# An attention and FFN kernel: tail keys as side-by-side 64-row matmuls, and the slot loop as one written-out list

## The chip, the cores and the metric

The kernel runs on one core of a Trainium2 chip. The metric is the device time of one execution in microseconds (us), lower is better. The core has TensorE (matrix products; the profile shows its weight loads apart, as PEld), VectorE (DVE), ScalarE (ACT), GpSimd (POOL) and SyncE (SP). POOL, SP and ACT also issue DMA transfers here. Each engine works through its own instructions in order and waits on semaphores for the others. TensorE reads SBUF and writes PSUM, eight banks of 2 KB per partition; ScalarE and VectorE read PSUM and write SBUF.

## What is computed

Self-attention over 8 batches and 8 heads of 576 tokens and 64 dimensions, with a bias that depends on the distance of two tokens, followed by a bilinear feed-forward network (FFN) over all 4608 tokens:

```
scores = q @ k.T / 8 + bias[|i - j|]          # per batch and head, 576 x 576
attn   = softmax(scores);  x = attn @ v       # back to [8*576, 512]
out    = ((x @ w_a) * (x @ w_b)) @ w_out      # 512 -> 1536 -> 512
```

## The kernel before

**Pairs and tails.** Two heads are worked together as a pair; pair p belongs to batch p // 4, so there are 32. The 576 tokens are four blocks of 128 ("main") and a tail of 64. Scores are made transposed, keys on partitions and queries along the free dimension. The bias enters as a product: `ex` (line 436) takes the exponential of the scores on ScalarE, and `mul` (442) multiplies it by the exponential of the bias on VectorE.

**Scores of a pair** (`qk`, line 408). For each main key block two products with 64 contracted rows, one per head, write the two banks of a `ps_sc` tile; there are two such tiles, used in turn, so a new block needs an older one to have been read by `ex`. For pairs from 8 on (`shared`), the call for blocks 2 and 3 also makes the scores of the tail queries against the main keys ("rows"), in eight 64-row products of 64 columns, into two banks: `trb`, otherwise used for transposes, and one of pool `ps_av`. `ex_rows` (428) reads them in two activations. `qk_tail` (484) makes the tail keys' scores in a third `ps_sc` tile: one product of 512 columns for the main queries and one of 128 for the tail queries. Its operand `z` holds the two heads as blocks on a diagonal, with zeros elsewhere, so that both heads go through all 128 rows at once. `ex_tail` (508) and `mul_tail` (526) follow.

**Products with V** (`av`, 559). The accumulators of a pair fit pool `ps_av`, one bank, in two rounds: query blocks 0 to 2, then block 3 and the tail. For each block, `av_mm` (563) first multiplies the tail keys' weights, both heads on 128 partitions, with `vt`, which is 130 columns wide and zero where head and partition do not match; then eight products of 65 columns over the main keys. For the query tail the main keys take four products of 130 columns. The 65th column of V is one, so that it sums the weights. `av_norm` (583) divides on VectorE into `XG`, and `t_x` (600) turns `XG` by DMA transposes on SP into `xn`, the FFN's input.

**FFN.** A chunk is 512 tokens. `ff_in` (639) makes `pa` or `pb`, four products of 512 columns; `ff_ha` copies `pa` out on ScalarE, `ff_g` multiplies it with `pb` on VectorE into `g`. `ff_o_mm` (673) makes a third of an output block in four products, `ff_o_out` (682) copies it out on ScalarE and issues its store from there. These go through the two banks of pool `ps_ff` in turn. A "unit" is one `ff_in` with what follows, or one third of an output block.

**Order of the work.** Every engine's instructions stand in the order in which the code issues them. Batches 0 and 1 (pairs 0 to 7) are in a written-out list, `opening` (737). From line 868, slots 8 to 32 follow: slot s makes the scores of pair s and the products with V of pair s - 1, and spreads nine FFN units over marks `U` between these steps. Loads of later batches are issued on POOL at fixed slots (`load_half`, `load_vt`), transposes of q and k on SP (`t_half`). What is left of the FFN follows the last slot. The chunk worked on lags the attention by a batch; the opening ends with the first three output units of chunk 0.

Of the kernel before, what the change touches and what calls it, by code (L numbers as in the profile page):

```python
# [13 lines left out]
def kernel(  # L14
# [33 lines left out]
    wrk = ctx.enter_context(tc.tile_pool(name="wrk", bufs=2))  # L48
    atp = ctx.enter_context(tc.tile_pool(name="atp", bufs=10))
    ps_sc = ctx.enter_context(tc.tile_pool(name="ps_sc", bufs=2, space=bass.MemoryType.PSUM))  # L50
    ps_av = ctx.enter_context(tc.tile_pool(name="ps_av", bufs=1, space=bass.MemoryType.PSUM))
    ps_tr = ctx.enter_context(tc.tile_pool(name="ps_tr", bufs=1, space=bass.MemoryType.PSUM))
    ps_ff = ctx.enter_context(tc.tile_pool(name="ps_ff", bufs=2, space=bass.MemoryType.PSUM))

    ctx.enter_context(tc.manual_schedule())

# [40 lines left out]
    tl = [wpool.tile([128, H // 2, 2, 128], BF16, name=f"tl{i}") for i in range(2)]  # L97
    vm = [wpool.tile([128, H, NM, Dh + 1], BF16, name=f"vm{i}") for i in range(2)]
    vt = [wpool.tile([128, 2, H // 2, Dh + 1], BF16, name=f"vt{i}") for i in range(2)]

    QT = [wpool.tile([128, NM, 128], BF16, name=f"QT{i}") for i in range(4)]
    KT = [wpool.tile([128, NM, 128], BF16, name=f"KT{i}") for i in range(4)]
# [69 lines left out]
    def load_vt(b):  # L172
        for hh in range(2):
            nc.gpsimd.dma_start(  # L174
                out=vt[b % 2][64 * hh:64 * hh + 64, hh, :, 0:Dh],
                in_=v[b, hh:H:2, SM:S, :].transpose([1, 0, 2]))

    def load_half(b, g):
# [37 lines left out]
    def pad_ones(i):  # L216
        nc.vector.memset(vt[i][0:64, 0, :, Dh:Dh + 1], 1.0)
        nc.vector.memset(vt[i][64:128, 1, :, Dh:Dh + 1], 1.0)
        nc.vector.memset(vm[i][:, :, :, Dh:Dh + 1], 1.0)

    def pad_x(i, eng):
        pad(eng, XG[i][64:128, 4, :, :], 64, 128)
# [182 lines left out]
    def shared(p):  # L405
        return p >= 8

    def qk(p, t0, ts=None):
        qT, kT, _ = operands(p)
        st[p].setdefault("at", [None] * NM)  # L410
        for t in ts or (t0, t0 + 1):
            ps = ps_sc.tile([128, 2, 512], FP32, tag="sc", name=f"qk{p}_{t}")
            for hh in range(2):
                r = slice(64 * hh, 64 * hh + 64)
                nc.tensor.matmul(out=ps[:, hh, :], lhsT=kT[r, t, :], rhs=qT[r, :, :],  # L415
                                 start=True, stop=True)
            st[p]["ps", t] = ps
        if shared(p) and t0 == 2:
            z = operands(p)[2]
            rows = (trb.bitcast(FP32), ps_av.tile([128, 512], FP32, tag="av", name=f"qr{p}"))  # L420
            for t in range(NM):
                for hh in range(2):
                    r = slice(64 * hh, 64 * hh + 64)
                    nc.tensor.matmul(out=rows[hh][:, ST * t:ST * t + ST], lhsT=kT[r, t, :],  # L424
                                     rhs=z[r, 0, ST * hh:ST * hh + ST], start=True, stop=True)
            st[p]["rows"] = rows

    def ex_rows(p):
        st[p]["att"] = at = att[p % 2]
        for hh in (1, 0):  # L430
            nc.scalar.activation(
                out=at[:, 0:512].rearrange("p (t h c) -> p h t c", h=2, t=NM)[:, hh, :, :],
                in_=st[p]["rows"][hh][:, 0:256].rearrange("p (t c) -> p t c", t=NM),
                func=ACTF.Exp, scale=scale)

    def ex(p, t):
        ps = st[p]["ps", t]
# [46 lines left out]
    def qk_tail(p):  # L484
        qT, kT, z = operands(p)
        ps = ps_sc.tile([128, 2, 512], FP32, tag="sc", name=f"qkt{p}")
        if shared(p):
            nc.tensor.matmul(out=ps[:, 0, :], lhsT=z[:, 1, :], rhs=qT[:, :, :], start=True, stop=True)  # L488
            nc.tensor.matmul(out=ps[:, 1, 0:2 * ST], lhsT=z[:, 1, :], rhs=z[:, 0, :],  # L489
                             start=True, stop=True)  # L490
            st[p]["ps"] = (ps, None)
            return
        for t in range(NM):
            nc.tensor.matmul(  # L494
                out=ps[:, 0, 2 * ST * t:2 * ST * t + 2 * ST],
                lhsT=kT[:, t, :], rhs=z[:, 0, :], start=True, stop=True)
        n = main_tail(p)
        nc.tensor.matmul(out=ps[:, 1, 0:n], lhsT=z[:, 1, :], rhs=qT[:, (SM - n) // 128:, :],
                         start=True, stop=True)
        pt = ps[:, 1, n:n + 2 * ST] if n < SM else tr_half().bitcast(FP32)[:, 0:2 * ST]  # L500
        nc.tensor.matmul(out=pt, lhsT=z[:, 1, :], rhs=z[:, 0, :], start=True, stop=True)  # L501
        st[p]["ps"] = (ps, pt)


    def main_tail(p):
        return SM // 2 if p < 4 else SM

    def ex_tail(p):
        ps, pt = st[p]["ps"]
        n = main_tail(p)  # L510
        at = att[p % 2]
        m = 512 + n
        st[p]["att"] = at
        if shared(p):
            nc.scalar.activation(out=at[:, 512:m + 2 * ST],  # L515
                                 in_=ps[:, :, :].rearrange("p a x -> p (a x)")[:, 0:SM + 2 * ST],
                                 func=ACTF.Exp, scale=scale)
            return
        if n < SM:
            m += 2 * ST  # L520
        else:
            nc.scalar.activation(out=at[:, m:m + 2 * ST], in_=pt, func=ACTF.Exp, scale=scale)
        nc.scalar.activation(out=at[:, 0:m], in_=ps[:, :, :].rearrange("p a x -> p (a x)")[:, 0:m],
                             func=ACTF.Exp, scale=scale)

    def mul_tail(p):
        if not shared(p):
            mul_rows(p)
        at, wt = st[p]["att"], Wt_sb[:, p % 4, :]
        o = 512 + main_tail(p) - 128  # L530
        nc.vector.tensor_tensor(out=at[:, o:o + 256], in0=at[:, o:o + 256], in1=wt[:, 255::-1], op=MULT)

    def mul_rows(p):
        at, w = st[p]["att"], W_sb[p % 4]
        x = at[:, 0:512].rearrange("p (t h c) -> p h t c", h=2, t=NM)
        rev = w[:, :, ST - 1::-1]
        e = bass.AP(tensor=rev.tensor, offset=rev.offset,
                    ap=[rev.ap[0], rev.ap[1], [1, NM], rev.ap[2]])
        nc.vector.tensor_tensor(out=x, in0=x, in1=e, op=MULT)

    def weights(p, t, hh, jq):
        if p >= 4:
# [2 lines left out]
        return st[p]["at", jq // 2, t // 2][:, hh, o:o + 128]  # L545

    def weights_last(p, t):
        return st[p]["att"][:, 2 * ST * t:2 * ST * t + 2 * ST]

    def weights_tail(p, jq):  # L550
        if jq == 4:
# [4 lines left out]
        o = 512 + 128 * (jq if p >= 4 else jq - 2)  # L556
        return st[p]["att"][:, o:o + 128]

    def av(p, jqs):
        av_mm(p, jqs)  # L560
        av_norm(p, jqs)

    def av_mm(p, jqs, pool=None, tag="av"):
        b, hp = divmod(p, 4)
# [298 lines left out]
    for token in opening.split():  # L863
        step(token)
    pad_tl(1)

    load_slot = {bb: 9 if bb == 3 else 12 if bb == 4 else 4 * bb - 5 for bb in range(3, B)}
    for s in range(8, NP + 1):
        new = s < NP
        U = "unit"  # L870
        A = lambda *jq: (lambda: av(s - 1, jq) if s > 8 else None)
        steps = []
        if new:
            steps += [lambda: (qk(s, 0), ex(s, 0))]
        if new:
            head = [U, lambda: ex(s, 1), A(0, 1, 2), U, lambda: mul(s, 0), U,
                    lambda: mul(s, 1)]
            late = [A(3, 4), lambda: t_x(s - 1), U]
            if s == 8:
                late = [U]  # L880
            pair = [lambda: v_next(s), lambda: (qk(s, 2), ex(s, 2), ex_rows(s)), U,
                    lambda: ex(s, 3), U, lambda: mul(s, 2), lambda: mul_rows(s)]
            tail = [lambda: (qk_tail(s), ex_tail(s)), U, U, lambda: mul_tail(s)]
            if s % 4 == 0:
                steps += head + late + [U] + pair + [lambda: mul(s, 3)] + tail
            else:
                steps += head + pair + late + [U, lambda: mul(s, 3)] + tail
        else:
            ff["late"] = True
            steps += [A(0, 1, 2), U, U, U, A(3, 4), lambda: t_x(s - 1, (0, 1, 2)), U, U, U,  # L890
                      lambda: t_x(s - 1, (3, 4)), U, U, U]
        b = s // 4 + 1
        if s % 4 == 2 and b < B:
            t_half(b, 0)
        if s % 4 == 0 and 2 <= b - 1 < B:
            t_half(b - 1, 1)
        if s % 4 == 1 and 2 <= b < B:
            load_vt(b)
        for bb in range(3, B):
            for g in range(2):  # L900
                if s == load_slot[bb] + (2 - (bb < 5)) * g:
                    load_half(bb, g)
        quota = 9
        seen, put = 0, 0
        nu = sum(1 for x in steps if x is U)
        for x in steps:
            if x is U:
                seen += 1
                n = (quota * seen + nu - 1) // nu - put
                put_units(n)  # L910
                put += n
            else:
                x()
    put_units(len(units) - nxt)


# [28 lines left out]
```

## Time and profile before

| | |
|---|---|
| time, median of 3 runs (lowest, highest) | 413.77 us (413.61, 414.19) |
| span of the profiled execution | 412.1 us |
| TensorE busy | 401.5 us, 97% |
| VectorE, ScalarE, GpSimd busy | 240.6, 252.0, 131.4 us |
| 896 products `av<-vm,at` of 65 columns (line 578) | 41.2 us |
| 152 products `av<-vt,att` of 130 columns (line 568) | 33.6 us |
| 128 products `av<-vm,att` of 130 columns (line 572) | 12.6 us |

The profile is of one execution. The page gives that execution's time as its span, from the first to the last instruction; the timed executions have some 1.7 us more around it. The page of a profile lists busy times and instruction counts by engine, the chain of work that ended last, and groups of instructions by line, engine and operands; a timeline lists instructions in order with their start and duration in us. A product's duration includes its way through the array after its last column, so that products one after another overlap in the records, and the distance of two starts is what one of them costs TensorE. Where two products are recorded as starting a few ns apart, they run together. A few matmul records are missing from the trace: 152 of the 160 tail products of line 568, for example.

### The profile page before, as it was taken

The numbers are of one execution on the slowest core, as the hardware profiler recorded it, in microseconds if no ns is written. First come the engines' busy times: TensorE is split into PE (matmuls) and PEld (weight loads), VectorE is DVE, ScalarE is ACT, GpSimd is POOL, SyncE is SP. The second block draws the span as 40 slices with busy tenths as digits, with TensorE's granted clock in tenths as the row PEclk, the third lists the DMA queues.
The fourth block names the chain that finished last, engine by engine and source line by source line (L and its number), as shares of the span: only waits on it lengthen the run. The fifth ranks groups of instructions, "written<-read, shape, count | busy, mean of one in ns | idle before, by whom it ended". The sixth has DMA issues, their size and how long they took to land.

```text
span 412.1 us, 8718 instructions
## 1 busy us (share of the span) xinstructions
PE 401.5 (97%) x3420; PEld 209.6 (51%) x3471; DVE 240.6 (58%) x568; ACT 252.0 (61%) x386; POOL 131.4 (32%) x188
## 2 busy tenths in 40 slices
PE   7999999999999999999999999999999999999996
PEld 3476656455554555455445555555445454444443
DVE  4799997366755765476646764567547652421320
ACT  5898992577748665667557765767476642322321
POOL 5966466887029400960069004300000000000000
PEclk9999999999999999999999999999999999999999
DMA  9999999999969924994199908960520012002004
GB/s 152 185 204 197 206 137 148 166 184 131 91 127 157 141 40 91 151 127 94 35 159 150 120 17 136 117 92 17 117 67 17 16 40 78 0 5 98 2 2 102
DMA packets 135962, 42.36 MB, mean 103 GB/s; under 512 B 113544, under 2 KB 131176, under 8 KB 135920
## 3 DMA queue, kind: packets, MB, share of 16 engines
q0 software_dynamic: 81120, 19.88, 54.9%
q1 hardware_dynamic: 49456, 12.61, 19.9%
q10 hardware_dynamic: 5344, 9.31, 7.1%
q8 instruction: 27, 0.44, 0.5%
q14 instruction: 15, 0.12, 0.1%
HBM read 39.23 MB, written 9.45 MB: 118 GB/s over the span
## 4 chain that ended last, share of the span: by engine, by line
PE 95%; DMA 1%; ACT 1%; issue 1%; DVE 0%; ACTq 0%; SPq 0%
PE pb L642 23%; PE pa L642 23%; PE po L679 22%; PE av L578 8%; PE qk L415 7%; PE av L568 2%; PE av L572 2%; PE qkh L455 1%; PE qkt L488 1%; DMA xn<-in_k_dram 1%; PE trb L330 1%; PE trb L424 1%; PE trk L330 1%; ACT ath L461 0%; PE qkt L494 0%
## 5 line engine op out<-in xcount | busy, mean ns | idle before, releaser
L439 ACT ACTIVATE at<-qk 128x1024 bf16<-128x1024 f32 x112 | 113.4, 1029 | 27.4 <-DMA out_dram<-ob 10.3
L652 DVE TENSOR_TENSOR g<-pb,ha 128x512 bf16<-128x512 f32 (+1 forms) x114 | 75.6, 663 | 74.8 <-PE pb L642 58.5
L642 PE MATMUL pb<-xn,wb 128*128 128x512 bf16 (+1 forms) x440 | 111.1, 368 | 0.8
L642 PE MATMUL pa<-xn,wa 128*128 128x512 bf16 (+1 forms) x440 | 110.8, 368 | 0.7
L649 ACT ACTIVATE ha<-pa 128x512 f32<-128x512 f32 (+1 forms) x114 | 66.3, 581 | 67.6 <-PE pa L642 63.8
L679 PE MATMUL po<-wo,g 128*128 128x512 bf16 x403 | 95.5, 379 | 0.8
L444 DVE TENSOR_TENSOR at<-at,W 128x1024 bf16<-128x1024 bf16 x112 | 75.0, 685 | 22.4 <-ACT at L439 22.3
L642 PEld LDWEIGHTS <-wa 128*128 128x128 bf16 x456 | 41.2, 98 | 46.6 <-issue 6.8
L642 PEld LDWEIGHTS <-wb 128*128 128x128 bf16 x456 | 40.6, 98 | 42.9 <-issue 4.7
L679 PEld LDWEIGHTS <-g 128*128 128x128 bf16 x420 | 38.8, 98 | 44.9 <-issue 2.5
L684 ACT ACTIVATE ob<-po 128x512 f32<-128x512 f32 x34 | 20.4, 600 | 40.2 <-PE po L679 30.1
L578 PE MATMUL av<-vm,at 128*128 128x65 bf16 x896 | 41.2, 193 | 0.0
L578 PEld LDWEIGHTS <-at 128*128 128x128 bf16 x896 | 37.4, 97 | 6.1
L174 POOL DMA_DIRECT2D vt<-in_v_dram x12 | 7.4, 622 | 101.9 <-PE av L572 101.1
L136 POOL DMA_DIRECT2D qn<-in_q_dram x48 | 36.6, 825 | 9.2 <-PE trb L501 6.9
L589 DVE RECIPROCAL rc<-av 128x6 f32<-128x6 f32 (+1 forms) x64 | 11.9, 186 | 45.7 <-PE av L578 41.1
L145 POOL DMA_DIRECT2D kn<-in_k_dram x48 | 36.2, 800 | 2.6 <-DMA qn<-in_q_dram 1.6
L568 PE MATMUL av<-vt,att 128*128 128x130 bf16 x152 | 33.6, 221 | 0.2
L415 PE MATMUL qk<-QB,KB 64*128 64x512 bf16 x192 | 29.1, 381 | 0.3
L591 DVE TENSOR_TENSOR XG<-av,rc 128x384 bf16<-128x384 f32 (+2 forms) x64 | 27.2, 425 | 2.2
L515 ACT ACTIVATE att<-qkt 128x640 bf16<-128x640 f32 x24 | 16.8, 701 | 13.0 <-PE qkt L489 13.0
L568 PEld LDWEIGHTS <-att 128*128 128x128 bf16 x152 | 14.9, 98 | 6.4
(105 smaller groups left out, 322.8 us busy)
## 6 DMA issues: line engine op xcount, KB each, us to landing
out_dram<-ob ACTq DMA_DIRECT2D x31, 256.0 KB, 2.9
vn<-in_v_dram POOLq DMA_DIRECT2D x16, 256.0 KB, 5.7
kn<-in_k_dram POOLq DMA_DIRECT2D x48, 64.0 KB, 4.9
qn<-in_q_dram POOLq DMA_DIRECT2D x48, 64.0 KB, 4.1
wa<-in_moe_w_a_dram POOLq DMA_DIRECT2D x3, 512.0 KB, 8.9
wb<-in_moe_w_b_dram POOLq DMA_DIRECT2D x3, 512.0 KB, 8.3
wo<-in_moe_w_out_dram POOLq DMA_DIRECT2D x1, 1536.0 KB, 15.7
xn<-XG SPq DMA_TRANSPOSE x52, 3.5
```

The lines of the kernel that those rows point to most:

```text
L136: nc.gpsimd.dma_start(out=by_tile(qn[b % 2])[:, h0 // 4, t, :, :], in_=q[b, h0:h1, 128 * t:128 * t + 128, :].transpose([1, 0, 2]))
L145: nc.gpsimd.dma_start(out=by_tile(kn[b % 2])[:, h0 // 4, t, :, :], in_=k[b, h0:h1, t:SM:NM, :].transpose([1, 0, 2]))
L415: nc.tensor.matmul(out=ps[:, hh, :], lhsT=kT[r, t, :], rhs=qT[r, :, :], start=True, stop=True)
L439: nc.scalar.activation(out=at[:, :, :], in_=ps[:, :, :], func=ACTF.Exp, scale=scale)
L444: nc.vector.tensor_tensor(out=at[:, :, :], in0=at[:, :, :], in1=w[:, :, S - 1 + t:S - 1 + t - SM:-1], op=MULT)
L568: nc.tensor.matmul(out=pav[:, slot, :, :], lhsT=weights_tail(p, jq), rhs=vt[i][:, :, hp, :], start=True, stop=True)
L578: nc.tensor.matmul(out=pav[:, slot, hh, :], lhsT=weights(p, t, hh, jq), rhs=vm[i][:, 2 * hp + hh, t, :], start=False, stop=True, skip_grou ...
L591: nc.vector.tensor_tensor(out=xg[:, jqs[0]:jqs[0] + m, :, :], in0=pav[:, 0:m, :, 0:Dh], in1=rc[:, 0:m, :].unsqueeze(3).to_broadcast([128, ...
L642: nc.tensor.matmul(out=ps[:, 0:n], lhsT=w[df // 4][:, mc, 128 * (df % 4):128 * (df % 4) + 128], rhs=xn_sb[mc][:, 512 * c + lo:512 * c + lo ...
L649: nc.scalar.activation(out=ha[:, 0:n], in_=ff["pa", df, lo][:, 0:n], func=ACTF.Copy)
L652: nc.vector.tensor_tensor(out=g_sb[df][:, lo:lo + n], in0=ff["pb", df, lo][:, 0:n], in1=ff["ha", df, lo][:, 0:n], op=MULT)
L679: nc.tensor.matmul(out=po[:, :], lhsT=g_sb[df][:, 128 * tt:128 * tt + 128], rhs=wo_sb[:, df, :], start=(df == 0), stop=(df == NDF - 1))
```

## The change

1. **Tail keys, pairs from 8 on.** The tails of V go to a buffer of their own, `vc`, in which each head has its 64 partitions and 65 columns, without zeros. `av_tails` makes the tail products as ten 64-row products of 65 columns, the two heads alternating, and `av_main` follows with 40 products of 65 columns over the main keys; the query tail's four products of 130 columns are now eight of 65. All five query blocks of both heads are accumulated in one round in `xav`, two banks, one for each head. `av_out` and `av_out_last` divide all of it: one reciprocal, one product and two small ones, where two rounds took six instructions.
2. **Rows.** The tail queries' scores against the tail keys leave `qk_tail` and join the rows as a fifth pair of 64-row products. The rows are made after the first two score blocks, not the last two, and read by one activation instead of two.
3. **Banks.** Pools `ps_av` and `ps_tr` are closed after the opening, and their two banks become the tile `xb`, which holds in turn the rows, the accumulators `xav` and, for the last pair, the transposes.
4. **Order.** The slot loop becomes a list of single steps over the four slots of a batch, `steady`, the same for batches 2 to 7. A token names a step and the slot within the batch: Q0 and Q2 score blocks (Q0 with the rows, Q2 with the tail products of the pair before), QZ the tail keys' scores, E, ER, EZ exponentials, M, MR, MZ products with the bias, AV, N, NT products with V and division of the pair before, X its transposes; FA, FB, HA, G, FO, HO the parts of FFN units. For chunk 0 the tokens FO0, FO1, FO2 and HO0 are passed over.

```diff
@@ qk, qk_tail, ex_rows
-        if shared(p) and t0 == 2:
+        if shared(p) and t0 == 0:
             z = operands(p)[2]
-            rows = (trb.bitcast(FP32), ps_av.tile([128, 512], FP32, tag="av", name=f"qr{p}"))
-            for t in range(NM):
+            for t in range(NM + 1):
                 for hh in range(2):
                     r = slice(64 * hh, 64 * hh + 64)
-                    nc.tensor.matmul(out=rows[hh][:, ST * t:ST * t + ST], lhsT=kT[r, t, :],
+                    nc.tensor.matmul(out=xb[:, hh, ST * t:ST * t + ST],
+                                     lhsT=z[r, 1, :] if t == 0 else kT[r, t - 1, :],
                                      rhs=z[r, 0, ST * hh:ST * hh + ST], start=True, stop=True)
...
-            nc.tensor.matmul(out=ps[:, 1, 0:2 * ST], lhsT=z[:, 1, :], rhs=z[:, 0, :],
-                             start=True, stop=True)
...
+    def av_tails(p):
+        b, hp = divmod(p, 4)
+        for jq in range(5):
+            for hh in range(2):
+                r = slice(64 * hh, 64 * hh + 64)
+                nc.tensor.matmul(out=xav[:, hh, jq, :], lhsT=st[p]["att"][r, 128 * jq:128 * jq + 128],
+                                 rhs=vc[b % 2][r, hp, :], start=(jq == 0), stop=True,
+                                 skip_group_check=True)
+
+    def av_main(p):
+        b, hp = divmod(p, 4)
+        for t in range(NM):
+            for jq in range(5):
+                for hh in range(2):
+                    nc.tensor.matmul(out=xav[:, hh, jq, :],
+                                     lhsT=weights(p, t, hh, jq) if jq < 4 else weights_last(p, t),
+                                     rhs=vm[b % 2][:, 2 * hp + hh, t, :], start=False, stop=True,
+                                     skip_group_check=True)
...
@@ slot loop
-        quota = 9
-        ...
+    steady = """
+        Q0.0 E0.0 FO0 FO1 QZ.0 E1.0 FO2 ER.0 M0.0 EZ.0 Q2.0 E3.0 E2.0 AV.0 N.0 NT.0 V.2 FO3 HO0 MR.0
+        M3.0 FO4 FO5 FO6 HO1 Q0.1 FO7 MZ.0 E0.1 E1.1 X.0 FO8 FO9 ER.1 FO10 FO11 M2.0 HO2 V.0 HO3
+        M1.0 FA0 FB0 HA0 G0 QZ.1 M1.1 FA1 FB1 EZ.1 HA1 G1 Q2.1 FA2 M0.1 FB2 HA2 E2.1 G2 M2.1 AV.1
+        E3.1 FA3 N.1 NT.1 HA3 FB3 Q0.2 FA4 E0.2 HA4 MZ.1 G3 FB4 X.1 QZ.2 FA5 E1.2 EZ.2 ER.2 G4 HA5
+        FB5 MR.1 Q2.2 FA6 M0.2 G5 MR.2 FB6 HA6 M3.1 AV.2 G6 E3.2 E2.2 M1.2 FA7 HA7 FB7 N.2 NT.2 Q0.3
+        G7 FA8 E0.3 HA8 FB8 E1.3 MZ.2 ER.3 QZ.3 M2.2 EZ.3 G8 FA9 X.2 HA9 FB9 M3.2 Q2.3 FA10 G9 FB10
+        MR.3 AV.3 HA10 E3.3 MZ.3 E2.3 M1.3 FA11 G10 N.3 NT.3 FB11 M0.3 X.3 M3.3 HA11 M2.3 G11
+    """.split()
...
+    for b in range(2, B):
+        c = b - 2
+        for token in steady:
+            kind, _, r = token.partition(".")
+            if r:
+                pair_step(kind, 4 * b + int(r))
+                continue
+            if token == "FA0":
+                c += 1
+            if c == 0 and token in ("FO0", "FO1", "FO2", "HO0"):
+                continue
+            ff_step(c, token)
+
+    p = NP - 1
+    ff["late"] = True
+    av_tails(p)
+    av_main(p)
+    put_units(1)
+    av_out(p)
+    put_units(1)
+    av_out_last(p)
+    put_units(2)
+    t_x(p, (0, 1, 2))
+    put_units(1)
+    t_x(p, (3, 4))
     put_units(len(units) - nxt)
```

## The prediction

> **What bounds the kernel now.** I read the page's busy shares first, then the chain that ended last, a table of stretches for the slot loop, the timeline of TensorE over one slot, and the timelines of TensorE and ScalarE at 73 us, where the slot loop begins.
>
> ```profile
> PE 401.5 (97%) x3420; PEld 209.6 (51%) x3471; DVE 240.6 (58%) x568; ACT 252.0 (61%) x386; POOL 131.4 (32%) x188
> PE 95%; DMA 1%; ACT 1%; issue 1%; DVE 0%; ACTq 0%; SPq 0%
> 180.00:200.00 20.00, 19.84 (x173) 9.91 (x175) 13.48 (x29) 14.12 (x22) 2.49 (x4) 1.00 0.64 81
> ```
>
> The third line is a stretch of the slot loop: TensorE 19.84 of 20.00 us at granted clock 1.00, VectorE 13.48, ScalarE 14.12. TensorE alone sets the time there: the first score products of two slots start at 116.18 and 127.19, 11.01 us apart. What the change is worth is what it takes off TensorE in a slot, less whatever idle time the new order opens. Busy time counts a product's drain too, so prices are start-to-start:
>
> ```profile
> 204.99 0.81 PE L679 MATMUL po<-wo,g 128*128 128x512 bf16 x3
> 205.63 0.22 PE L568 MATMUL av<-vt,att 128*128 128x130 bf16 x1
> 205.69 0.42 PE L578 MATMUL av<-vm,at 128*128 128x65 bf16 x8
> 205.95 0.22 PE L568 MATMUL av<-vt,att 128*128 128x130 bf16 x1
> ...
> 210.22 0.59 PE L679 MATMUL po<-wo,g 128*128 128x512 bf16 x2
> 210.74 0.60 PE L415 MATMUL qk<-QB,KB 64*128 64x512 bf16 x4
> 211.19 0.19 PE L424 MATMUL trb<-ZB,KB 64*128 64x64 bf16 x1
> 211.19 0.19 PE L424 MATMUL qr<-ZB,KB 64*128 64x64 bf16 x1
> ...
> 211.27 0.19 PE L424 MATMUL trb<-ZB,KB 64*128 64x64 bf16 x1
> 211.28 0.19 PE L424 MATMUL qr<-ZB,KB 64*128 64x64 bf16 x1
> 211.40 1.90 PE L679 MATMUL po<-wo,g 128*128 128x512 bf16 x8
> 213.14 0.38 PE L488 MATMUL qkt<-QB,ZB 128*128 128x512 bf16 x1
> 213.35 0.22 PE L489 MATMUL qkt<-ZB 128*128 128x128 bf16 x1
> 213.41 0.38 PE L679 MATMUL po<-wo,g 128*128 128x512 bf16 x1
> ```
>
> A 130-column tail product takes 0.06 (205.63 to 205.69), the eight 65-column ones after it (205.95 - 205.69) / 8 = 0.0325 each, a 512-column one 0.215. A pair of 64-row products takes (211.27 - 211.19) / 3, about 0.029, for two products and two weight loads: they run side by side. Going from 128 rows to 64 costs 0.09 (last po at 210.43, streamed out by 210.65, qk at 210.74), and going back 0.09 (211.28 + 0.03 to 211.40). The 128-column product takes 0.06 (213.35 to 213.41).
>
> **The change, part by part.**
>
> 1. *TensorE work of a slot.* Before, the products with V run 0.95 (queries 0 to 2: 205.63 to 206.59) and 0.61 (208.31 to 208.92): 1.56 us. They are 5 tail products, 32 of 65 columns, and 4 of 130 for the query tail. After, the 4 become 8 of 65, so 40 x 0.0325 = 1.30; the tails become 5 pairs, 5 x 0.029 = 0.15. In the scores, the 128-column product (0.06) becomes a fifth pair (0.03). The tails follow the second score products and the rows the first, which already are 64-row stretches, so a slot keeps two switches each way. Saving: 1.56 + 0.06 - 1.30 - 0.15 - 0.03 = 0.14 us a slot, times 24 slots = 3.4 us. The split of the query tail gives nothing: 4 x 0.0575 = 0.23 becomes 8 x 0.0325 = 0.26. Bounds: if the tail and row pairs cost two full loads of 0.0325 each, the slot gains -0.07 (1.7 us lost in all); if the 40 products ran at the pair's 0.029, it gains 0.28 (6.7 us). I take 3.4, since both rows have the very shapes.
>
> [...]
>
> 2. *The first slot, 8.* In the steady order two or three FFN pieces (0.86 us each) stand between Q0, QZ and Q2. In slot 8 the first three, FO0 to FO2, are skipped because the opening has done them, so QZ follows the row scores directly, and Q2 follows QZ. Both need a scores bank that ScalarE must first read out (two banks in turn). The lines of before:
>
> ```profile
> 73.72 0.61 PE L415 MATMUL qk<-QB,KB 64*128 64x512 bf16 x4
> 74.26 4.49 PE L679 MATMUL po<-wo,g 128*128 128x512 bf16 x19
> ```
> ```profile
> 73.82 0.60 ACT L684 ACTIVATE ob<-po 128x512 f32<-128x512 f32 x1 [3.74 <-PE po L679]
> 74.45 0.38 ACTq L687 DMA_DIRECT2D out_dram<-ob  x1
> 74.88 1.94 ACT L439 ACTIVATE at<-qk 128x1024 bf16<-128x1024 f32 x2 [0.46 <-ACT ob L684]
> ```
>
> Before, the nineteen FFN products from 74.26 cover the exponentials. After, TensorE could start QZ at 74.40, but E0 starts behind the output copy and its DMA issue at 74.88, ends at 75.90, and is seen 0.05 later (an ath of the opening ends at 24.73, the qkt that waits for it starts at 24.78): idle 1.55. QZ ends at 76.17, the switch at 76.26; E1 ends at 76.82, seen at 76.87: idle 0.61. The first pair of Q2 ends at 77.09; the second needs EZ, which stands behind ER: ER from 76.73 for 0.70 (the 640-element row of line 515), EZ from 77.34 for 0.60 (the 512-element row of line 684), done 77.94, seen 77.99: idle 0.90. Sum 3.05 us, once. If ER costs 0.77, as the two activations of line 431 do, 3.1; if the issue of 0.38 were away, 2.7.
>
> 3. *The last pair.* After slot 31 there is no next score block: pair 31's tails make their own switch (+0.1 with what overlapped before), and the order leaves M2 last on VectorE. From the end A of the products of pair 30, VectorE does reciprocal, normalization, two small ones, M0, M3, M2: 0.20 + 0.22 + 0.61 + 0.47 + 0.60 + 0.60 + 0.68, so at A + 3.4 us (steps from the starts 332.81, 333.02, 333.23, 333.70 and a pitch of 0.60 in two M; normalization from 0.29 at 128 and 0.56 at 384 elements, 0.69 at 512). TensorE has two FFN pieces (1.73), the tails (0.33) and two of four quarters (0.65), so A + 2.7: idle 0.7. Nothing else covers it; bounds 0.5 to 0.9. With the switch, 0.8.
>
> 4. *Inside the steady order.* Each hand-over by hand, 0.04 per semaphore and 0.16 from a 512-column product's streaming end to its result: FB0 needs the bank that HO3 frees: 0.16 + 0.04 + 0.60 + 0.04 = 0.84 after FO11, while FA0 covers 0.86: 0.02 to spare. FB1 needs G0: 0.16 + 0.04 + 0.69 + 0.04 = 0.93 after FB0; QZ and FA1 cover 1.08. ScalarE work falls (0.38 + 0.39 + 0.70 to 0.70 + 0.60), VectorE's too. I take 0.2 us in all for six blocks; bounds 0 and, with four hand-overs a block late by 0.1 each, 2.4.
>
> 5. *Queues.* POOL: the V tails go to a buffer of their own, so the second load_vt no longer waits (3.73 us before 71.09) and batch 3's loads go out that much sooner; they share the DMA with the transposes of batch 2, of which ZB (issued 65.72) is now needed at 74.2, not 79.1; a landing up to 75.7 hides behind E0, one at the 10 us that a transpose took at worst (75.7) still does. The later waits of 17 to 27 us stay, now on the tail products. SP: the pair's transposes now stand behind the next batch's KB, QB, ZB ones. The urgent one, X.0, can go at 6.7 us into its block (N done) and FA0 comes at 14.1: 7.4 us, against landings of 2.4 to 5.7 in the loop and 7.8 at worst in the opening, where it would cost 0.4 a block. Nothing. Two more start-up memsets lie in VectorE's 0.7 us wait for bl_sb. Nothing.
>
> **Sum.** -3.4 + 3.05 + 0.8 + 0.2 = +0.65 us. The profiled span is 412.1 us; the median of the three runs is 413.77, so 1.7 lie around the span, unchanged. 412.1 + 0.65 + 1.7 = 414.4 us: no change. About 0.2%, 0.83 us, is what a measurement of this kernel tells from no change (412.94 to 414.60).
>
> **Rivals.**
>
> *The steady order stalls (the other side).* One mechanism: hand-overs to the two FFN banks come late, since FA0, FB0 and FB1 have 0.02 to 0.15 to spare by my sums. Against it: before, ScalarE's ha starts 0.04 after its product in most rows. For it: 67% and 71% busy engines in strict order. At 2.4 us in place of 0.2 the time is 416.6; it decides for slower from 0.4 us in all, under 0.02 a slot.
>
> *The saving is larger.* If the 40 products, alternating two banks, ran at 0.029: 413.77 - 6.7 + 4.05 = 411.1. Against it: the fourth-to-fifth product before already changes its target without running faster.
>
> *The change doesn't do what it says.* Tail pairs not side by side: 413.77 + 1.7 + 4.05 = 419.5. Line 424 speaks against it.
>
> **How the numbers follow.** Forecast, 413.0 to 414.6: 0.40. Stalls in the steady order, or slot 8 dearer by late data: 0.37. Larger saving, or slot 8's idle time shorter: 0.18. Not side by side: 0.05. So faster 0.18, same 0.40, slower 0.42. The range 411.6 to 417.4 leaves out about 0.1 on each side: most of the pairs' failure and long stalls above, the full 0.029 below.
>
> **What would show it.** Pitch 0.0325 in the products with V and 0.029 a pair in the tails; a slot of 10.87 us; TensorE idle near 74.4, 76.3 and 77.1; a gap of 0.7 before the last pair's third quarter; no DMA among TensorE's waits. Wrong if the slots differ from 10.87 by more than 0.05, or if slot 8 shows no idle time.

## The result: 0.36% slower

The changed kernel takes 415.36 us (median of 7 runs, 414.58 to 415.65), the kernel before 413.77 (413.61 to 414.51, 7 runs): a ratio of 1.0036, 95% interval 1.0023 to 1.0048. The forecast was 414.4, no change; the time lies inside the range given and in the case "slower", to which the prediction gave 0.42. Run once more beside the last experiments, the changed kernel took 414.88 (ratio 1.0023, 1.0008 to 1.0039).

The page of the profile after, busy shares and chain, and the same stretch of the slot loop as before:

```profile
PE 399.2 (96%) x3656; PEld 207.7 (50%) x3711; DVE 233.6 (56%) x522; ACT 250.3 (61%) x362; POOL 131.3 (32%) x188
PE 91%; DMA 4%; DVE 2%; ACT 1%; issue 1%; ACTq 0%; SPq 0%
```
```profile
180.00:200.00 20.00, 19.84 (x212) 10.24 (x208) 13.14 (x28) 14.28 (x20) 4.81 (x8) 1.00 1.12 102
```

TensorE is busy 2.3 us less than before (401.5), and in the loop it is as full as before. But the span grew from 412.1 to 413.7, and a DMA has come into the chain: 4%, where it was 1%. So the work got cheaper, and idle time took more than that back. The timeline of TensorE in a steady slot (start, duration, line, operands, count) shows the cheaper work:

```profile
103.43 0.32 PE L566 MATMUL xb<-vc,att 64*128 64x65 bf16 x10
103.68 1.04 PE L676 MATMUL pa<-xn,wa 128*128 128x512 bf16 x3
...
105.42 0.41 PE L575 MATMUL xb<-vm,at 128*128 128x65 bf16 x8
...
106.64 0.81 PE L676 MATMUL pa<-xn,wa 128*128 128x512 bf16 x3
```

Ten tail products with the switch take 103.68 - 103.43 = 0.25 us, 40 products with V 106.64 - 105.42 = 1.22. Four slots, from Q0 of slot 12 to Q0 of slot 16, take 43.18 us where they took 44.02 (two rows of the profile before, then two of the one after):

```profile
116.18 0.60 PE L415 MATMUL qk<-QB,KB 64*128 64x512 bf16 x4
160.20 0.60 PE L415 MATMUL qk<-QB,KB 64*128 64x512 bf16 x4
```
```profile
118.39 0.61 PE L418 MATMUL qk<-QB,KB 64*128 64x512 bf16 x4
161.57 0.61 PE L418 MATMUL qk<-QB,KB 64*128 64x512 bf16 x4
```

That is 0.21 a slot, 24 x 0.21 = 5.0 us saved. The loss is in slot 8 (same view):

```profile
74.33 0.61 PE L418 MATMUL qk<-QB,KB 64*128 64x512 bf16 x4
77.11 0.20 PE L426 MATMUL xb<-ZB 64*128 64x64 bf16 x2 [2.17 <-DMA ZB<-tl]
...
78.71 0.39 PE L418 MATMUL qk<-QB,KB 64*128 64x512 bf16 x2 [0.64 <-ACT att L514]
79.27 5.08 PE L713 MATMUL po<-wo,g 128*128 128x512 bf16 x15 [0.17 <-issue]
84.28 0.61 PE L418 MATMUL qk<-QB,KB 64*128 64x512 bf16 x4
```

The row scores wait for ZB until 77.11, the second pair of Q2 waits for EZ, and then fifteen recorded FFN products (the record of the first one is missing) take 84.28 - 79.27 = 5.0 us, the switch to the next Q0 included, where 15 x 0.216 + 0.09 = 3.3 would do. In the table of stretches, the granted clock is the third number from the end:

```profile
75.83:79.25 3.42, 1.35 (x15) 0.61 (x17) 1.46 (x3) 2.90 (x5) 3.42 (x5) 1.00 2.27 185
79.25:82.66 3.41, 3.39 (x8) 1.22 (x8) 2.44 (x5) 1.83 (x2) 2.13 (x4) 0.50 1.81 137
```

For one piece of 3.41 us, right after a piece in which TensorE was busy for 1.35 us, the clock is half, and eight products take 0.427 us each. That costs 3.41 / 2 = 1.7 us. From Q0 of slot 8 to Q0 of slot 12 the trace has 44.06 us. A steady block has 43.18; without the three output pieces (12 x 0.216 = 2.6) and without the products with V that block 2 does not have to do (1.22 and about 0.16) it would be 39.2. So slot 8 loses about 4.9 us.

### The profile page after: what moved, and what is told of

The parts are those of the page before. It is cut to its first block, busy times and chain, and to the rows that moved or that the text cites. A ratio compares the mean times of both kernels' runs of the same rounds, so it can differ in the third digit from the quotient of the medians.

```text
span 413.7 us, 9142 instructions
## 1 busy us (share of the span) xinstructions
PE 399.2 (96%) x3656; PEld 207.7 (50%) x3711; DVE 233.6 (56%) x522; ACT 250.3 (61%) x362; POOL 131.3 (32%) x188
## 4 chain that ended last, share of the span: by engine, by line
PE 91%; DMA 4%; DVE 2%; ACT 1%; issue 1%; ACTq 0%; SPq 0%
PE pb L676 22%; PE pa L676 22%; PE po L713 22%; PE qk L418 7%; PE xb L575 7%; DMA ZB<-tl 3%; PE av L612 2%; PE qkh L456 1%; PE qkt L489 1%; DMA xn<-in_k_dram 1%; PE xb L426 1%; PE xb L566 1%; PE trb L333 1%; PE trk L333 1%; PE av L602 1%
## 5 line engine op out<-in xcount | busy, mean ns | idle before, releaser
L440 ACT ACTIVATE at<-qk 128x1024 bf16<-128x1024 f32 x112 | 110.1, 1022 | 19.5 <-PE qk L418 18.9
L676 PEld LDWEIGHTS <-wb 128*128 128x128 bf16 x456 | 43.6, 98 | 50.3 <-issue 2.1
L575 PEld LDWEIGHTS <-at 128*128 128x128 bf16 x768 | 30.6, 97 | 5.3 <-DVE at L445 0.8
L575 PE MATMUL xb<-vm,at 128*128 128x65 bf16 x768 | 31.9, 193 | 0.6 <-DVE at L445 0.4
L176 POOL DMA_DIRECT2D vc<-in_v_dram x12 | 7.5, 632 | 78.0 <-PE xb L566 76.0
L575 PE MATMUL xb<-vm,att 128*128 128x65 bf16 x192 | 21.4, 193 | 0.0
L462 ACT ACTIVATE ath<-qkh 128x1024 bf16<-128x1024 f32 x16 | 16.0, 1024 | 2.7 <-PE qkh L456 2.5
L432 ACT ACTIVATE att<-xb 128x640 bf16<-128x640 f32 x24 | 17.1, 713 | 0.0
L584 DVE TENSOR_TENSOR XG<-xb,rc 128x512 bf16<-128x512 f32 x24 | 16.6, 692 | 0.8
L418 PEld LDWEIGHTS <-KB 64*128 64x128 bf16 x192 | 5.6, 94 | 21.1 <-issue 21.1
```

The costliest lines, as they stand in the source:

```text
L432: nc.scalar.activation(out=at[:, SM:].rearrange("p (t h c) -> p h t c", h=2, t=NM + 1), in_=xb[:, :, 0:320].rearrange("p h (t c) -> p h t ...
L440: nc.scalar.activation(out=at[:, :, :], in_=ps[:, :, :], func=ACTF.Exp, scale=scale)
L575: nc.tensor.matmul(out=xav[:, hh, jq, :], lhsT=weights(p, t, hh, jq) if jq < 4 else weights_last(p, t), rhs=vm[b % 2][:, 2 * hp + hh, t, : ...
L676: nc.tensor.matmul(out=ps[:, 0:n], lhsT=w[df // 4][:, mc, 128 * (df % 4):128 * (df % 4) + 128], rhs=xn_sb[mc][:, 512 * c + lo:512 * c + lo ...
```

## The experiments

All are compared with the kernel before on the same chip; the names in brackets are used below. A difference between two experiments can also be one between two sessions, in which the kernel before had medians of 413.77 to 414.04 us. Theory 1 puts the loss into slot 8 and the last pair, theory 2 (the rival of the prediction) into hand-overs in all slots.

**Cover in slot 8 (e1).** The nine output pieces that chunk 0 has left take the first nine of the twelve positions, not the last nine.

```diff
-            if c == 0 and token in ("FO0", "FO1", "FO2", "HO0"):
-                continue
+            if c == 0 and token[1] == "O":
+                i = int(token[2:]) + (3 if token[0] == "F" else 1)
+                if i > (11 if token[0] == "F" else 3):
+                    continue
+                token = token[:2] + str(i)
```

> The changed kernel (415.4 us) with one edit: for chunk 0 the positions FO0 to FO8 take the nine output pieces that are left (3 to 11) and the last three positions stay empty, where the change leaves the first three empty. So slot 8 has two FFN pieces before QZ and one before Q2; the row scores stay in Q0. Theory 1, all of the loss lies in slot 8 (late ZB 2.3 us, missing cover before Q2 0.8, half clock after the idle stretch 1.7): the wait for ZB stays, about 2.3 us at 74.8; no wait for EZ before the second pair of Q2, and no FFN product at 0.427 us, since the idle stretch is one of 2.3 us. Up to 0.5 us comes back where FB0 of chunk 1 now follows HO3 more closely. 412.8 to 413.5 us; 414.5 if 2.3 us of idle time are enough for the half clock. Theory 2, the loss is spread over the steady order of all slots: 415.4 us, no change.

412.11 us (409.82 to 415.34, 12 runs), ratio 0.9964 (0.9935 to 0.9993): 3.3 us less than the changed kernel, 0.7 below the range expected, and below the kernel before. In the profile, block 2 takes 41.78 in place of 44.06 us; ZB is still waited for (2.17), EZ no more. The twelve times fall into two groups, eight from 409.8 to 412.7 and four from 414.8 to 415.3. The profiled one is of the first and has no half clock after its idle stretch:

```profile
74.73:78.15 3.42, 1.51 (x16) 0.81 (x17) 1.45 (x3) 2.64 (x3) 3.42 (x6) 1.00 1.79 176
78.15:81.56 3.41, 3.41 (x18) 1.31 (x17) 0.07 (x2) 1.71 (x3) 2.17 (x5) 1.00 1.62 172
```

The four upper runs have a mean granted clock of 0.994 to 0.996, as every run of the changed kernel in the first comparison. That they lost a piece at half clock in slot 8 is likely but not shown: no profile of them was taken, and the mean clock alone does not sort the runs, as three of the eight lower ones have 0.990 or 0.991. A mean that low can come from the start, where the profile of e9 (0.992) has half clock from 7.83 to 14.65 us.

**The clock alone (e2).** Nine products of zeros fill slot 8's wait; nothing else moves and no wait goes.

```diff
+        if p == 8 and t0 == 0:
+            warm_up(9, ps_ff.tile([128, 512], FP32, tag="ffn", name="fill8"))
         if shared(p) and t0 == 0:
```

> The changed kernel with nine 512-column products of zeros (9 x 0.216 = 1.9 us, to a spare FFN bank, result not used) between the score products and the row scores of slot 8. All waits of slot 8 stay as they are: rows for ZB until about 77.1 us, then those for E0 and EZ. Theory 1 (TensorE is given half the clock after some 4 us with little work): the eight FFN products after 79 us take 0.216 us each in place of 0.427, granted clock 1.00 there, 415.4 - 1.7 = 413.7 us. Rival (those products are slow for another reason, such as the copies, stores or loads beside them): still 0.427 us, 415.4 us.

414.00 us (413.27 to 416.12), ratio 1.0009 (0.9994 to 1.0024): 1.4 us less than the changed kernel's first median, 0.9 less than its second. ZB is there at 77.05, EZ is waited for as before, and the sixteen FFN products take 3.56 us:

```profile
78.69 0.39 PE L418 MATMUL qk<-QB,KB 64*128 64x512 bf16 x2 [0.68 <-ACT att L516]
79.02 3.63 PE L715 MATMUL po<-wo,g 128*128 128x512 bf16 x16
```

Same waits, more work, less time: the slow products come from the idle stretch, and cost what the clock says. Two of the eleven runs, 415.56 and 416.12 us at mean clocks of 0.998 and 1.000, are long for a reason that the record does not show. Block 2 fell by 1.8 us, to 42.23.

**The order of the products with V (e3, e4).** The change has key block, query block, head. First head, query block, key block, then key block, head, query block:

```diff
-        for t in range(NM):
-            for jq in range(5):
-                for hh in range(2):
+        for hh in range(2):
+            for jq in range(5):
+                for t in range(NM):
```
```diff
-            for jq in range(5):
-                for hh in range(2):
+            for hh in range(2):
+                for jq in range(5):
```

> The changed kernel with the 40 products with V of a pair in the order head, query block, key block: four in a row add to the same target and twenty in a row go to one bank, as in the kernel before. The time falls out by the pitch of these products, 0.030 us in the changed kernel and 0.0325 in the kernel before. Theory A, a product that adds to the target of the one just before it costs 2.5 ns more: 0.0325 us for three in four, 24 x 30 x 0.0025 = +1.8, 417.2 us. Theory B, two banks in turn are what makes it shorter: 0.0325 us for nearly all, 24 x 40 x 0.0025 = +2.4, 417.8 us. Theory C, the order does not matter and the shorter pitch has another source: 415.4 us. Besides, the quarters of M2 and M3 are needed earlier; that may add a wait of some 0.1 to 0.3 us in a slot, which the list of waits would show apart.

> The changed kernel with the 40 products with V of a pair in the order key block, head, query block: five in a row go to one bank, no two in a row to the same target. Theory A (a repeated target costs 2.5 ns): pitch 0.030, 415.4 us. Theory B (two banks in turn make it shorter): 0.0325 for four in five, 24 x 32 x 0.0025 = +1.9, 417.3 us.

e3: 416.85 us (ratio 1.0067, 1.0050 to 1.0084); e4: 414.29 (1.0016, 1.0004 to 1.0029). In e3 the 40 products take 106.20 - 104.92 = 1.28 us, and four slots 43.41; in e4 four slots take 43.17, as in the change:

```profile
104.92 0.67 PE L575 MATMUL xb<-vm,at 128*128 128x65 bf16 x16
105.43 0.29 PE L575 MATMUL xb<-vm,att 128*128 128x65 bf16 x4
105.56 0.68 PE L575 MATMUL xb<-vm,at 128*128 128x65 bf16 x16
...
106.20 1.03 PE L676 MATMUL pa<-xn,wa 128*128 128x512 bf16 x4
```

So two banks in turn are not it (theory B falls), and the order is. Theory A, the repeated target, gives the right sum but not the right places. Averaged over 22 pairs of e3, from the second query block on, the first product of a block takes 29.0 to 29.2 ns and the next three 32.1 to 33.8, as A says; but the first product of the second head, whose target is new too, takes 32.6, and so does the fifth of each eight in the kernel before (32.4, 89 groups). Those two read the V block that lies directly behind the last one, as the products inside a group of four do. In the changed kernel, where no two products in a row have the same target, eight of the 40 still take 33 to 36 ns. Whether the target, the order of the V operands or something else sets the 3 ns stays open.

**The two heads in turn in the kernel before (b1).** Its only edit:

```diff
-            for hh in range(2):
-                for t in range(NM):
+            for hh, t in [(x, y) for y in range(NM) for x in range(2)] if p >= 8 else [(x, y) for x in range(2) for y in range(NM)]:
```

> The kernel before (413.9 us) with one edit: for pairs from 8 on the eight 65-column products with V of a query block go key block by key block with the two heads in turn, so no two in a row add to the same target; they stay in one bank, and the tail products stay as they are. Theory A (a repeated target costs 2 to 2.5 ns): pitch 0.0305 in place of 0.0325, 24 slots x 32 products x 0.002 = -1.5, 412.3 us. Rival (the pitch in the changed kernel came from the side-by-side tails or the banks): 413.9 us.

412.00 us, ratio 0.9955 (0.9942 to 0.9967). Eight products now take 0.24 in place of 0.26 us:

```profile
204.58 0.40 PE L577 MATMUL av<-vm,at 128*128 128x65 bf16 x8
204.82 0.22 PE L568 MATMUL av<-vt,att 128*128 128x130 bf16 x1
```

Four slots fall from 44.02 to 43.78, 24 x 0.06 = 1.4 us of the 1.9; in the two profiles, the rest is slot 8's start, 73.26 after 73.72. The fourth and the sixth of eight still take 32 to 33 ns, the others 29, which neither the target nor the order of V by itself explains. One line does more for the kernel before than the whole change did.

**Tails not alternating (e6).** Five products on the upper 64 rows, then five on the lower.

```diff
-        for jq in range(5):
-            for hh in range(2):
+        for hh in range(2):
+            for jq in range(5):
```

> The changed kernel (415.4 us) with the ten tail products of a pair in the order head, query block: five on the upper 64 rows, then five on the lower, in place of alternating. Theory A (a pair costs 0.029 us because its two products lie on different row halves and stand next to each other): each product now costs what one costs by itself, 0.029 to 0.0325 us, so ten cost 0.29 to 0.33 in place of 0.15: +0.15 to +0.18 a slot, 24 slots, 419.0 to 419.7 us. Rival (64-row products of 65 columns are short in any order): 0.015 us each, 415.4 us.

416.93 us, ratio 1.0063 (1.0043 to 1.0082). The ten products with the switch take 0.29 us, against 0.25:

```profile
103.56 0.36 PE L566 MATMUL xb<-vc,att 64*128 64x65 bf16 x10
103.85 1.04 PE L676 MATMUL pa<-xn,wa 128*128 128x512 bf16 x3
```

That is 0.04 a slot, about 1 us in all; neither 0.15 to 0.18 nor nothing. All ten start within 0.17 us, at distances that fit two sets of five running beside each other, the second begun 0.04 us after the first; the records do not name the half of the rows, so this is a reading. By it, side by side did not need neighbours in the list here, only something left to overlap. The rest of the time is not separated further: this profile has two pieces of half clock in slot 8 (76.83 to 83.66) and one late hand-over.

**Rows later, and the end (e8).** With the cover, the row scores of slot 8 go behind its first two pieces, and one output piece stands between the tails and the products with V of pair 31.

```diff
-        if shared(p) and t0 == 0:
+        if p > 8 and t0 == 0:
+            qk_rows(p)
...
         elif kind == "QZ":
+            if s == 8:
+                qk_rows(s)
             qk_tail(s)
...
     av_tails(p)
-    av_main(p)
     put_units(1)
+    av_main(p)
     av_out(p)
```

> The kernel with the covered slot 8 (output pieces 3 to 11 in positions FO0 to FO8, 412.1 us median, in two groups of runs: 409.8 to 412.7 and 414.8 to 415.3), with two edits more: the row scores of slot 8 stand behind its first two FFN pieces, just before QZ, and after slot 31 one output piece stands between the tails of pair 31 and its other products with V. Theory 1 (slot 8's loss is late ZB, missing cover and the half clock that follows a window with little work): the wait for ZB shrinks from 2.2 us to 0.0 to 1.2, no window of TensorE is emptier than half, so the upper group of runs is gone; the wait for M2 in the last pair (0.6 us) is gone too. 409.0 to 410.5 us, in one group. Theory 2 (the upper group has another cause than the idle stretch): still two groups, some runs near 414.

410.80 us (410.05 to 412.31, 6 runs, one group), ratio 0.9930 (0.9912 to 0.9948): faster than both kernels, 0.3 above the range expected. The line "emptier than half" was the author's estimate; the pieces measured put it near 1.5 of 3.41 us (last section). TensorE in slot 8 and in the last pair:

```profile
74.61 1.90 PE L716 MATMUL po<-wo,g 128*128 128x512 bf16 x8
77.03 0.20 PE L429 MATMUL xb<-ZB 64*128 64x64 bf16 x2 [0.53 <-DMA ZB<-tl]
...
331.97 0.41 PE L578 MATMUL xb<-vm,at 128*128 128x65 bf16 x8
332.21 0.22 PE L578 MATMUL xb<-vm,att 128*128 128x65 bf16 x2
332.27 0.41 PE L578 MATMUL xb<-vm,at 128*128 128x65 bf16 x8
```

Block 2 takes 40.25 us, 1.0 over the 39.2 worked out above. From Q0 of slot 31 to the end it is 88.43 us, against 89.35 in the changed kernel: the last pair had cost 0.9.

**An order of its own for block 2 (e9)**, with three pieces ahead of the rows, and the end as in e8.

```diff
+    first = """
+        Q0.0 E0.0 FO3 FO4 FO5 E1.0 HO1 QR.0 QZ.0 ER.0 FO6 M0.0 EZ.0 Q2.0 E3.0 E2.0 V.2 MR.0 M3.0
+        FO7 FO8 HO2 Q0.1 FO9 MZ.0 E0.1 E1.1 FO10 FO11 ER.1 M2.0 V.0 HO3 M1.0
+    """.split() + steady[steady.index("FA0"):]
...
-        for token in steady:
+        for token in first if b == 2 else steady:
```

> The changed kernel with the end as in the run before this one, and block 2 with an order of its own up to FA0: Q0, E0, three output pieces (FO3 to FO5), E1, HO1, then the row scores, QZ, ER, FO6, EZ, Q2, and later FO7, FO8, HO2, Q0 of slot 9, FO9, FO10, FO11, HO3. Theory 1: three pieces (2.6 us) cover a ZB that lands as late as 77.0 us, so the wait for it is at most 0.3; EZ may hold up the second pair of Q2 by up to 0.3; no half clock. All that the steady order saves (24 slots x 0.21 = 5.0 us) then remains: 413.9 - 5.0 + 0.3 = 409.2 us, 408.7 to 409.8. Theory 2 (the steady order loses elsewhere too): 411 us or more.

410.93 us (410.17 to 412.01), ratio 0.9929 (0.9914 to 0.9944), about 1.7 more than expected. ScalarE's timeline says where its profiled run lost 2.25 us: the issue of HO1's store stood in its queue until 79.31, and ER and EZ, which Q2 needs, behind it. By the trace's records the issue waited for a semaphore that a transpose (`xn<-XG`, issued at 70.76, landed at 79.23) was to raise, and the store's own landing is told by the same one: in the records the two share a semaphore, not data.

```profile
76.30 0.60 ACT L721 ACTIVATE ob<-po 128x512 f32<-128x512 f32 x1 [0.32 <-PE po L716]
79.31 0.37 ACTq L724 DMA_DIRECT2D out_dram<-ob  x1
79.78 0.70 ACT L435 ACTIVATE att<-xb 128x640 bf16<-128x640 f32 x1 [2.88 <-DMA xn<-XG]
```

**KB earlier on SP (e10, e11).** e11 is e8 with this edit, e10 is e9 with it and with HO1 moved:

```diff
+        elif kind == "TB":
+            nc.sync.dma_start_transpose(
+                out=KB[0][:, 0, :, :, :].rearrange("d t h c -> d (t h) c"), in_=kn[0][:, 0:1024])
         elif kind == "TH":
-            t_half(2, 0)
+            t_half(2, 0, ((QB, qn),))
...
-        CQ6:A AV40 N40 FA5b S71 E71 S73 MT5 M50 FB5b HA5b AV41 S72 E73 G5b N41 M71 FA6f M73 T6 E72 M72
+        CQ6:A AV40 N40 FA5b S71 E71 S73 MT5 M50 FB5b HA5b AV41 S72 E73 G5b TB N41 M71 FA6f M73 T6 E72 M72
```
```diff
-        Q0.0 E0.0 FO3 FO4 FO5 E1.0 HO1 QR.0 QZ.0 ER.0 FO6 M0.0 EZ.0 Q2.0 E3.0 E2.0 V.2 MR.0 M3.0
+        Q0.0 E0.0 FO3 FO4 FO5 E1.0 QR.0 QZ.0 ER.0 FO6 M0.0 EZ.0 Q2.0 E3.0 E2.0 HO1 V.2 MR.0 M3.0
```

> The kernel with block 2 in an order of its own (410.9 us median), with two edits. First, HO1 stands behind E2, not behind E1: its store's issue on ScalarE stood 2.9 us for a transpose, with ER and EZ behind it, and held up the second pair of Q2 by 2.25 us. Second, the KB transpose of batch 2 goes out on SP before the transposes of pair 4, about 1.4 us of SP issue time taken out from ahead of ZB. Theory 1 (ZB lands when the transposes ahead of it are through): ZB lands 1.0 to 1.4 us earlier, near 75.7 us, no wait for it behind three pieces; no wait over 0.3 us at Q2; no half clock in the slot loop: 410.9 - 2.3 - 0.6 = 408.0, with the spread of the opening 408.0 to 409.3 us. Theory 2 (the loads on POOL, not SP's order, set ZB's landing): the wait for ZB stays at some 0.7, 408.6 to 409.9.

> The kernel with covered slot 8, row scores behind two pieces and the fixed end (410.8 us median, wait for ZB 0.5 us at 77.0) with the early KB transpose alone. Theory 1 (SP's order sets ZB): rows start at 76.2 to 76.5 without a wait for ZB, 410.3 us. Theory 2 (the loads set it): wait 0.5 us as before, 410.8 us.

412.58 us (410.82 to 414.69; ratio 0.9980, 0.9960 to 1.0000) and 412.07 (411.15 to 415.32; 0.9969, 0.9948 to 0.9989): no gain, losses of 1.7 and 1.3 against e9 and e8. In e10, HO1's new place took the wait at Q2 away, and neither kernel waits for ZB any more; but the transpose moved ahead stood on SP until 56.42 and 58.04 us, and pair 4's transposes, at 54.44 and 54.05 in the two profiles of the changed kernel, came after it. XG was free later, and TensorE waited in the opening instead (the list of its waits in e11: us in total, times, longest):

```profile
PE av L605 <- DVE XG L628: 2.6, 2, 1.6
```

Slot 8 began at 76.71 and 76.16 us, 2 us late, and the rows, at 79.94 and 78.53, come after 77.3, where the latest wait for ZB in these profiles ends. So these two do not tell whether SP's order or the loads set ZB's landing. They show what an early place in a queue costs when the data are not there. In e10 the new idle stretch was also followed by half clock, from 69.45 to 72.87 us.

**HO1 and HO3 moved, SP as it was (e13).** HO1 as in e10, and:

```diff
-        FO7 FO8 HO2 Q0.1 FO9 MZ.0 E0.1 E1.1 FO10 FO11 ER.1 M2.0 V.0 HO3 M1.0
+        FO7 FO8 HO2 Q0.1 FO9 MZ.0 E0.1 E1.1 FO10 FO11 HO3 ER.1 M2.0 V.0 M1.0
```

> The kernel with block 2 in an order of its own (410.9 us median, second pair of Q2 held up 2.25 us by EZ behind HO1's store issue) with the transposes in their old order on SP, HO1 behind E2, and HO3 ahead of the row exponentials of slot 9. Theory 1 (ScalarE's queue held up Q2, nothing else in slot 8): wait before the second pair of Q2 under 0.1 us, wait for ZB 0 to 0.7, FB0 waits 0.3 us for HO3 in place of 0.9, no half clock between 60 and 100 us: 410.9 - 2.25 + 0.3 = 409.0, with the spread of the opening 408.5 to 410.3 us. Theory 2 (the time of slot 8 is set by DMA whatever the order): 410.9 us, as the two versions before.

410.73 us (409.88 to 411.15, 5 runs), ratio 0.9913 (0.9899 to 0.9927). There is no wait for ZB, none at Q2 and no half clock after 60 us; FB0 waits 0.27 for HO3, and FA1 0.37 for HA0, which now stands behind ER. The mechanism was as expected, the time was not: 0.4 above the range. Block 2 takes 40.44 us, not less than in e8, and the two can't be told apart.

**The changed kernel again, as it is (e12).**

> The changed kernel as it is, for its spread beside these runs. Theory 1 (slot 8 loses about 4.8 us: wait for ZB 1 to 3 us as ZB happens to land, 0.6 for EZ, 1.7 for one window of half clock): the profile shows the half clock in the 3.4 us after the idle stretch again, the wait for ZB between 1.0 and 3.0 us; 414.0 to 415.7 us.

414.88 us (413.17 to 416.06, 12 runs), ratio 1.0023 (1.0008 to 1.0039). The second profile has the wait for ZB (2.59 us, until 77.13) and half clock from 78.94 to 82.36. Block 2 takes 44.43.

## Why the prediction was right and wrong

The range held, and the forecast, no change, missed a loss of 0.36%. That it came so near is partly luck: the saving was forecast 1.6 us too small and the loss in slot 8 some 1.8 us too small, and the two misses nearly cancel. By its own sign, "wrong if the slots differ from 10.87 by more than 0.05", the prediction was wrong on the slots, which take 43.18 / 4 = 10.80 us. Step by step:

1. *TensorE work of a slot: -0.14 forecast, -0.21 measured; 3.4 became 5.0.* The tail pairs were right: 0.25 with the switch, where 5 x 0.029 and 0.09 make 0.24. The lower bound and the rival "not side by side", two full loads of 0.0325 to a pair, were the author's estimate: with the switch the ten would have taken 10 x 0.0325 + 0.09 = 0.42. The term that was mis-sized is "40 x 0.0325 = 1.30", which measured 1.22. The row had the very shape but another order, and the order is worth 2 to 3 ns a product: e3 gives it up, and b1 gives it to the kernel before. The argument against the larger saving ("the fourth-to-fifth product before already changes its target without running faster") was true and did not bear: a new target alone does not do it (32.4 ns for that product).
2. *Slot 8: 3.05 forecast, about 4.9 measured.* That QZ and Q2 would come too early for ScalarE was right. The first FFN product has no record; it began near 79.04, if it came 0.33 us after the second pair of Q2 as in e2 (79.02 - 78.69). From 74.33 to then TensorE had 1.5 us of work by the prices of the prediction, so idle time was about 3.2 us, near the 3.05, though its first part, forecast as 1.55 for E0, was 2.2 for ZB. In e3's profile ZB came at 75.5, and its waits are those forecast, shrunk by the one for ZB in front: E0 0.31, E1 0.54, EZ 0.69. "A landing up to 75.7 hides behind E0" did not help, as ZB did not land by then: its issue went out at 66.45, not 65.72, and it was there at 77.1, 10.7 us later, where 10 had been taken as the worst. Where the profiles of this family show a wait for ZB, it ends between 75.5 and 77.3. The missing term is the clock: half speed for 3.41 us after the idle stretch, 1.7 us. Stretches of 3 us were summed as if TensorE came out of them as it went in.
3. *The last pair: 0.8 forecast, 0.9 measured.* M2 came last, as said:

```profile
335.97 0.42 PE L575 MATMUL xb<-vm,at 128*128 128x65 bf16 x8 [0.42 <-DVE at L445]
```

One output piece ahead of the products with V takes the 0.9 back (e8). The wait listed is only a part of it.

4. *Steady order: 0.2 forecast, nothing measured.* Four slots take 43.18 us on average over blocks 3 to 6, and no wait of TensorE is listed there. The rival "the steady order stalls" did not happen, though FB0 had only the 0.02 to spare by the prediction's sums; theory 2 falls with e8, which left the steady order alone.
5. *Queues: nothing forecast.* In the steady slots TensorE waited for no DMA, as said, but the line "no DMA among TensorE's waits" failed in slot 8. Two readings of this step were off. Batch 3's loads of k went out on POOL at 72.92 us, not sooner than the 72.30 of before, as POOL waited for earlier loads instead. And the transposes that took 7.8 and 6.2 us to land, at 91.22 and 103.1, lie in the slot loop, not in the opening; no wait came of that.

With the measured terms the sum is -5.0 + 4.9 + 0.9 = +0.8 us; the spans differ by 1.6. Most of the rest is the opening: slot 8 began at 74.33 us, before at 73.72. Over the twelve profiles whose opening has the same order, that start lies between 72.96 and 74.55, with 73.72 and 73.26 in the two of the old slot loop, so it is not put down to the change. The clock has a part in it. In ten of these profiles the first full clock is recorded at some moment between 15.73 (b1) and 18.07 us (e2), in the changed kernel's first profile at 17.81 and before at 17.31; TensorE is slow until then (before, four products of 256 columns take 0.54 us from 15.90 and 0.33 from 17.98). The later that moment, the later slot 8 begins, by about 0.5 us per us (a straight line through the ten points; correlation 0.92), as half speed would have it. For the two kernels that is 0.25 of the 0.61 us.

## What to carry to other kernels

Look at the first turn of a steady order apart from the others: there the pieces that cover a wait may be missing, and it may need data earlier than the old loop did. Count idle time on TensorE by where it lies, not only by its sum, since here a piece of 3.41 us with 0.63 to 1.50 us of TensorE work in it was followed by one at half clock, which lost up to 1.7 us more (last section). And before restructuring products, try their order: one line in the kernel before gave 0.45%, where the whole change lost time and, mended, gave 0.7 to 0.9% with such an order in it.

## What the hardware showed that was not expected

In the profiles the granted clock changed only between 1.00 and 0.50, and each half-clock piece recorded is 3.41 us long, or two in a row, but for the last, which the end of the record cuts. All changes of one profile lie on a grid of 3.413 us: in the changed kernel's first profile 17.81, 79.25 and 82.66 us, 18 pieces ((79.25 - 17.81) / 18 = 3.413) and one piece apart. In the piece before half clock in the slot loop or just ahead of it, TensorE was busy by the records for 0.63 (e4), 1.17 (the changed kernel's second profile), 1.19 (e10), 1.33 (e6), 1.35 (its first) or 1.50 us (e3); after 1.51 (e1), 1.89 and 2.00 us (e9) the clock stayed full. The first and last microseconds do not fit so sharp a line: half clock followed a piece with 1.67 us in e10 (4.60 to 8.01), and full clock one with 1.47 us in e11 (404.96 to 408.38). A piece already at half clock is another case: in e6 one with 2.44 us (76.83 to 80.24) was followed by a second. For the slot loop at full clock the limit is thus estimated near 1.5 us of 3.41, not resolved further, as busy time by the records holds each product's drain (a 512-column product is recorded with 0.38 us, where starts are 0.216 apart). One long wait was not needed: in e3 no single wait listed in slot 8 is over 1.0 us, and the clock was halved all the same.

Products of 65 columns took from 29 to 36 ns, and reordering the same products moved their mean between 30.5 and 32 ns. By their starts, two sets of 64-row products on different halves of the rows overlapped even when issued one set after the other (e6: ten in 0.29 us with the switch, where 10 x 0.029 and 0.09 would be 0.38).
